# Moving half of a weight's decode from the last first product into the attention loop

## The chip, the cores and the metric

The kernel runs on one core of a Trainium2 chip. The metric is the device time of one execution in microseconds (us), as a median over several runs. The core has a matmul engine (PE, with its weight loads shown as PEld), a vector engine (DVE), an activation engine (ACT), a general engine (POOL) and a queue engine (SP), which here issues all the DMA transfers. The engines run side by side, each works through its own list in order, and they wait for each other by semaphores. Matmuls write into PSUM; everything else lies in SBUF, and the large intermediates lie in device memory.

## The reference

Thresholded attention (8 batches, 8 heads, 576 positions, head size 64), then a gated two-layer product over its output (4608 rows of 512, inner width 2048):

```python
scores = scale * np.matmul(q, k.transpose(0, 1, 3, 2))
thresh = np.max(scores, axis=-1, keepdims=True) - tau
scores = np.where(scores >= thresh, scores, -1000000000.0)
attn = np.exp(scores - np.max(scores, axis=-1, keepdims=True))
attn = attn / (np.sum(attn, axis=-1, keepdims=True) + 1e-09)
x = np.matmul(attn, v)      # heads side by side: (4608, 512)
h = x @ w_in                # (4608, 2048)
sp = np.where(h > 20.0, h, np.log1p(np.exp(np.minimum(h, 20.0))))
g = h * np.tanh(sp)
out = g @ w_out             # (4608, 512)
```

The function from `h` to `g` is Mish, which ACT has as one function. The two weights reach the chip as 64-bit floating-point numbers, viewed as integers, and are turned into 32-bit ones on the chip.

## The kernel before, in words

**Splitting.** Most products are made of 32-bit numbers split into a high part `hi`, rounded by ACT, and a low part `lo = x - hi`, subtracted by DVE or POOL. A product then takes three matmuls: high by high, high by low, low by high.

**Decode** (class `Decode`, lines 111 to 150). A piece of a weight is 128 rows by 256 columns (`WC`). `load` fetches the 64-bit words, 256 KB. `first` makes two ACT steps of 256 columns; `clamp` and `shift` are one DVE step each; `sign` is a third one on DVE; `add` is an integer add on POOL. Then the value is whole. `upper` rounds it to the high half (ACT), `lower` subtracts (DVE or POOL). `w_in` has 32 pieces, `w_out` has 32 as well: 16 rows of pieces (`NF`), two column halves.

**The attention loop** (from line 528) goes over 288 tiles of 128 rows of scores (`NT`), nine to a pair of heads. In its step `g` it issues, for each engine in the order in which the lines stand:
- `begin(g + 1)`: the score matmuls of the next tile, into one of two PSUM buffers `s`
- the products with `v` of an earlier tile, and ACT's copies of tile g - 3 (`evacuate_hi`)
- on DVE `row_max` of tile g, small steps, `lo_main` of tile g - 3, and, where g is even, `tail_lo`
- on ACT the exponential
- on POOL `normalise` of tile g - 1
- on DVE `masked`, the last reader of the PSUM buffer of scores of tile g, which the scores of tile g + 2 need
- `advance(stream, n)`: n matmuls of the first product (`x @ w_in`) of the batch before, n by the tables `MIX...`
- `transposes(g - 2)`.

Work that isn't tied to a tile is put into this order by lists. `weights` holds the pieces of `w_in`; in the steps that `W1_STEPS` names a piece is taken into `decoding`, and from then on each step issues its next entry: two empty ones (`LAG`), `first`, then the entries that `spread` lays out by `STAGES`, then `upper` and `lower`. An entry of three has its first part issued behind `lo_main`, its second ahead of `masked`, its third behind `masked` (from tile 39 on, `JOIN`). The 32 pieces of `w_in` are all taken by step 48. InOrder (line 77) keeps the order of each engine as written.

**The first product** (`gemm1`, line 440) makes `h` for half a batch (288 columns) and 128 inner rows in twelve matmuls, into one of two PSUM buffers shared with the products with `v`. A copy brings it to `hst`, four of them go to device memory in one store (`hd`); there are two `hst` buffers. For the batches ahead of the last, ACT copies; for the last batch (B - 1), DVE. After the last tile five steps of the loop drain (`DRAIN` matmuls of the product in each).

**The last first product** (lines 661 to 717) stands behind the loop. It has 32 units of 12 matmuls (`UNIT`, 384 in all). `decode_step(u)` is called ahead of each unit and issues the steps of all 32 pieces of `w_out`, a piece a unit, six pieces in flight. Four of the six homes lie in the large buffer `four`, two in small ones. In units 9, 11, 13 and 15 a quarter of `h` of chunk 0 (256 columns) goes through `gate`: ACT's Mish, ACT's rounding, POOL's subtraction, of 1024 columns each. Large buffers come from a pool of four of 16 KB (`slot`), small ones from a pool of two of 4 KB (`small`).

**The second product** (from line 737) goes over ten chunks of columns of `h`, the first and the last shorter, and in each over four output blocks `d` (`o`, 48 matmuls each); `d` 0 and 1 need the first column half of `w_out`, 2 and 3 the second. While a chunk is multiplied, the next ones are loaded and gated (`make_g`). Its matmuls aren't bound to the written order, and some of the first chunk's are placed among those of the last first product.

Of the kernel before, what the change touches and what calls it, by code (L numbers as in the profile page):

```python
# [7 lines left out]
U32 = mybir.dt.uint32  # L8
# [8 lines left out]
NP = H // 2  # L17
LOADS = ((1, 0, 1, 3, 2, 3, 7, 3, 5, 8), (0, 3, 3, 2, 5, 4, 5, 8, 5, 7), (0, 0, 2, 4, 5, 4, 7, 6, 7, 8))
W1_STEPS = (1, 3, 4, 6, 7, 8, 10, 12, 13, 15, 16, 17)
STAGES = ((0, 1, 1), (0, 1, 1))  # L20
THIRD = ((),)
LAG = 2
XSPLIT = (4, 1, 2)
# [11 lines left out]
HB = S // 2  # L35
NBLK = 2 * B
NC = 512
CHUNKS = (0, *range(256, B * S, NC), B * S)
QCOL = {
    0: [(0, 0)],  # L40
# [20 lines left out]
MIX = (11, 12, 6, 9, 8, 13, 12, 14, 16, 6, 16, 4, 12, 4, 15, 5, 16, 13)  # L61
MIX_FIRST = (11, 12, 6, 9, 8, 13, 6, 14, 22, 6, 16, 4, 12, 4, 15, 9, 16, 13, 7, 12, 5, 10, 8, 13, 12, 14, 16, 6, 16, 4, 12, 4, 15, 5, 16, 13)
MIX_LAST = (12, 14, 16, 6, 16, 4, 12, 4, 15, 5, 16, 13, 11, 12, 6, 9, 8, 13, 12, 14, 16, 6, 16, 4, 12, 4, 15, 5, 16, 13, 11, 12, 6, 9, 8, 13)
DRAIN = 24
LAST = {1: 0, 4: 1, 6: 2, 8: 3}
WIDTH = (256, 320, 320, 256)
XOFF = (0, 256, 256, 0)
# [85 lines left out]
def attention_moe(tc, q, k, v, tau, w_in, w_out, out):  # L153
# [3 lines left out]
    with ExitStack() as outer:  # L157
        dram = outer.enter_context(tc.tile_pool(name="dram", bufs=1, space=DRAM))
        cst = outer.enter_context(tc.tile_pool(name="cst", bufs=1, side="left"))
        psh = outer.enter_context(tc.tile_pool(name="psh", bufs=2, space=PSUM))  # L160
        hd = [dram.tile([P, NF, HB], F32, name=f"hd{i}") for i in range(NBLK)]

        ident = cst.tile([P, P], F32, name="ident")
# [6 lines left out]
        with ExitStack() as first:  # L170
# [6 lines left out]
            with ExitStack() as att:  # L177
# [11 lines left out]
                def spread(work, steps):  # L189
                    middle = [[skip] * 3 for _ in range(steps[2] + 1)]  # L190
                    for i, made in enumerate((work.clamp, work.shift, work.join)):
                        middle[steps[i]][i] = made
                    return middle

                def decode_w1(d, j):
                    sl = slice(j * WC, (j + 1) * WC)
                    st = dec.tile([P, 4 * WC], U32, name="dec")
                    half, at = divmod(j * WC, DF // 2)
                    hi, lo = (w[:, d, at:at + WC] for w in w1[half])
                    work = Decode(nc, st, hi, lo)  # L200
                    work.load(w_in[d * P:(d + 1) * P, sl])
                    if d + j * ND in ONV:
                        middle = [skip] * 3
                        middle[ONP] = lambda: work.lower(nc.vector)
                        last = [(work.upper,), middle]
                    else:
                        last = [(lambda: (work.upper(), work.lower(nc.gpsimd)),)]
                    return [(work.first, skip), *spread(work, STAGES[(d + j) % 2]), *THIRD, *last]

                def prep(pi):  # L210
                    full = pi < FULL
# [228 lines left out]
                def gemm1(b, xs):  # L440

                    halves = (range(NF // 2), range(NF // 2, NF))
                    if b < B - 1:
                        order = [(c, fs) for c in range(2) for fs in halves]
                    else:
                        order = [(c, fs) for fs in halves for c in range(2)]
                    for c, fs in order:
                        for f in fs:
                            h = psh.tile([P, 512], F32, name="h", tag="ph")
                            half, at = divmod(f * P, DF // 2)  # L450
                            i = 0
                            for d in range(ND):
                                xh, xl = xs[d][c]
                                wh, wl = (w[:, d, at:at + P] for w in w1[half])
                                for a, m in ((wh, xh), (wh, xl), (wl, xh)):
                                    nc.tensor.matmul(h[:, :HB], a, m, start=i == 0, stop=i == 3 * ND - 1)
                                    i += 1
                                    if i < 3 * ND:
                                        yield
                            if f % 4 == 0:  # L460
                                hst = xpool.tile([P, 4, HB], F32, name="hst", bufs=2)
                            if b < B - 1:
                                nc.scalar.copy(hst[:, f % 4], h[:, :HB])
                            else:
                                nc.vector.tensor_copy(hst[:, f % 4], h[:, :HB])
                            if f % 4 == 3:
                                nc.sync.dma_start(hd[2 * b + c][:, f - 3:f + 1, :], hst)
                            yield
# [5 lines left out]
                NPAIRS = B * NP  # L474
                NT = NPAIRS * 9
                weights = [lambda d=d, j=j: decode_w1(d, j) for j in range(DF // WC) for d in range(ND)]
                decoding = []
                pairs = {}
                tiles = {}
# [48 lines left out]
                for g in range(NT + 5):  # L528
# [71 lines left out]
                        chores.setdefault(max(g + 2, 2), []).append(work())  # L600
                    if weights and g % 18 in W1_STEPS:
                        decoding.append([()] * LAG + weights.pop(0)())
                    if g < NT:
                        if g < JOIN:
                            for work in now:
                                if len(work) == 3:
                                    work[2]()
                        if g % 2 == 0:
                            both = sm.tile([P, 2 * S], F32, name="p", bufs=2)
                        tiles[g]["both"] = both  # L610
                        half = both[:, :S] if g % 2 == 0 else both[:, S:]
                        tiles[g]["p"] = masked(g, tiles[g]["s"], tiles[g]["st"], tiles[g]["e"], half)
# [20 lines left out]
            def slot(pool, shape, kind, n):  # L633

                return pool.tile(shape, kind, name="g", tag="g", bufs=n)

            def small(kind, shape):
                return wr.tile(shape, kind, name="ht", tag="ht", bufs=2)

            def load_h(ht, c, fs):  # L640

                at, end = CHUNKS[c], CHUNKS[c + 1]
                while at < end:
                    i, off = divmod(at, HB)
                    m = min(HB - off, end - at)
                    to = at - CHUNKS[c]
                    nc.sync.dma_start(ht[:, :, to:to + m], hd[i][:, fs, off:off + m])
                    at += m
# [6 lines left out]
            def quarter(k):  # L655
                return slice(4 * k, 4 * k + 4)
# [3 lines left out]

            n0 = CHUNKS[1]
            w2 = [weights2(wr, 0)]
            four = slot(wr, [P, 4, 4 * WC], U32, 4)
            h0 = slot(wr, [P, NF, n0], F32, 4)
            g0 = [slot(wr, [P, NF, n0], F32R, 4) for _ in "hl"]
            work = {}

            def fetch(i):
                if i < 2 * NF:
                    st = four[:, i % 6] if i % 6 < 4 else small(U32, [P, 4 * WC])  # L670
                    work[i] = Decode(nc, st, None, None)
                    j, f = divmod(i, NF)
                    work[i].load(w_out[f * P:(f + 1) * P, j * WC:(j + 1) * WC])

            def decode_step(u):

                if (i := u - 3) in work:
                    work[i].first()
                if (i := u - 5) in work:
                    j, f = divmod(i, NF)  # L680
                    work[i].hi, work[i].lo = (w[:, f] for w in w2[j])
                    work[i].upper()
                if (i := u - 4) in work:
                    work[i].clamp()
                    work[i].shift()
                    work[i].sign()
                    work[i].add()
                if (i := u - 5) in work:
                    work.pop(i).lower(nc.vector if i % 2 else nc.gpsimd)
                    fetch(i + 6)  # L690

            for i in range(6):
                fetch(i)
            for k in range(4):
                load_h(h0[:, quarter(k)], 0, quarter(k))
            for _ in stream:
                pass
            stream = gemm1(B - 1, batches[B - 1])
            UNIT = 12
            for u in range(NF * 2):  # L700
                if u == NF + 2:
                    early.close()
                    er = second.enter_context(tc.tile_pool(name="er", bufs=1, side="right"))
                    w2.append(weights2(er, 1))
                decode_step(u)
                if u in (9, 11, 13, 15):
                    k = (u - 9) // 2
                    gate(h0[:, quarter(k)], *(g[:, quarter(k)] for g in g0), nc.gpsimd)
                if u == NF + 2:
                    h1 = slot(wr, [P, 8, NC], F32, 4)  # L710
                    for k in range(2):
                        load_h(h1[:, quarter(k)], 1, quarter(k))
                advance(stream, UNIT)
            for u in range(NF * 2, NF * 2 + 5):
                decode_step(u)
            for _ in stream:
                pass

# [83 lines left out]
```

## Time and profile before

| | us |
|---|---|
| median of 3 runs | 1405.22 |
| the runs | 1408.76, 1405.22, 1402.37 |
| the profiled execution | 1407.83 |
| its span (first to last instruction) | 1406.0 |

The mean granted clock of PE over the span is 0.982 of full speed.

| engine | busy us | share | instructions |
|---|---|---|---|
| PE | 1370.3 | 97% | 8798 |
| DVE | 1008.2 | 72% | 2992 |
| ACT | 947.1 | 67% | 2098 |
| POOL | 774.1 | 55% | 1107 |

A row of the timeline has the start in us, the length in us, the engine, the line (L87 is a helper through which all instructions of the ordered engines pass, so they are told apart by the names of their tiles), the operation, what is written from what is read, the shapes, and how many in a row were merged. In brackets stands for how long the engine had been idle, and what released it. Names in the trace: `g` and `ht` are also the homes of the pieces of `w_out`, since they come from those two pools; `dec` are the homes of pieces in the loop; `w2h` and `w2l` are the split second weight; `p<-s,st,e` on DVE is `masked`.

### The profile page before, as it was taken

What the parts mean: (1) busy time and instruction counts of PE and PEld (TensorE: products, weight loads), DVE (VectorE), ACT (ScalarE), POOL (GpSimd) and SP (SyncE); (2) the same over time, 40 slices, a digit from 0 to 9 for tenths busy, and PEclk for the clock granted to TensorE, in tenths of its full rate; (3) what the DMA queues carried; (4) which work ended last, traced back from release to release, by engine and by line L of the source; (5) the groups of instructions that cost most, each with busy time, mean ns of one, the idle gap of its engine ahead of it and who ended that gap; (6) DMA issues with size and microseconds to landing.
All of it is one profiled execution on the core that took longest, in us unless ns stands there. A gap on an engine that the chain in (4) does not pass through costs nothing.

```text
span 1406.0 us, 27557 instructions
## 1 busy us (share of the span) xinstructions
PE 1370.3 (97%) x8798; PEld 1234.7 (88%) x8798; DVE 1008.2 (72%) x2992; ACT 947.1 (67%) x2098; POOL 774.1 (55%) x1107
## 2 busy tenths in 40 slices
PE   8999899999999999999999999988899999999999
PEld 5555789999999999999999999987888888888888
DVE  4899999999999999999999999949934222322210
ACT  3778878888888888888888888746655333433310
POOL 3678888788788787787787887636500000000000
PEclk6999899999999999999999999998999999999999
DMA  4334323233333233232333332155656334544210
GB/s 131 90 89 114 111 83 122 91 108 105 99 96 113 91 117 108 91 117 91 112 101 100 99 113 88 59 200 160 207 148 164 116 112 121 143 109 116 83 53 29
DMA packets 121599, 154.62 MB, mean 110 GB/s; under 512 B 23152, under 2 KB 100976, under 8 KB 121456
## 3 DMA queue, kind: packets, MB, share of 16 engines
q1 hardware_dynamic: 121456, 152.87, 35.8%
q8 instruction: 70, 1.15, 0.3%
q14 instruction: 73, 0.60, 0.1%
HBM read 105.64 MB, written 47.19 MB: 109 GB/s over the span
## 4 chain that ended last, share of the span: by engine, by line
PE 88%; DVE 5%; ACT 3%; DMA 2%; issue 2%; POOL 0%; SPq 0%; POOLq 0%; ACTq 0%; DVEq 0%
PE o L751 27%; PE h L87 25%; PE s L87 14%; PE y L87 12%; PE tp L87 9%; PE t L87 1%; DVE g L87 1%; DVE st L87 1%; DVE p L87 1%; DVE ht L87 1%; DVE dec L87 1%; DMA g<-hd 1%; DMA g<-w_out 1%; ACT e L87 1%; DVE hst L87 0%
## 5 line engine op out<-in xcount | busy, mean ns | idle before, releaser
L751 PE MATMUL o<-g,w2h 128*128 128x512 f32 (+1 forms) x1280 | 367.5, 372 | 1.9 <-POOL g L87 1.9
L87 PE MATMUL h<-xh,w1h 128*128 128x288 f32 x1024 | 305.2, 298 | 9.2 <-DVE hst L87 8.3
L87 PE MATMUL h<-xl,w1h 128*128 128x288 f32 x1024 | 304.8, 298 | 0.5 <-POOL xl L87 0.5
L87 PE MATMUL h<-xh,w1l 128*128 128x288 f32 x1024 | 304.5, 297 | 0.0
L87 POOL TENSOR_SCALAR p<-p,st 128x576 f32<-128x576 f32 x288 | 245.0, 851 | 66.5 <-DVE st L87 40.4
L751 PEld LDWEIGHTS o<-g,w2h 128*128 128x128 f32 x1280 | 234.1, 190 | 45.7 <-POOL g L87 2.1
L87 PE MATMUL s<-k,q 128*128 128x288 f32 (+1 forms) x1280 | 260.2, 329 | 12.2 <-DVE p L87 10.8
L87 DVE SCALAR_TENSOR_TENSOR p<-s,st,e 128x576 f32<-128x576 f32 x288 | 235.0, 816 | 23.5 <-ACT e L87 13.8
L751 PE MATMUL o<-g,w2l 128*128 128x512 f32 (+1 forms) x640 | 238.2, 372 | 3.7 <-POOL w2l L87 3.7
L87 ACT ACTIVATE e<-s,st 128x576 f32<-128x576 f32 x288 | 214.4, 744 | 36.1 <-DVE st L87 29.0
L87 DVE TENSOR_REDUCE st<-s 128x1 f32<-128x576 f32 x288 | 216.5, 752 | 12.1 <-PE s L87 12.0
L87 PEld LDWEIGHTS s<-k,q 128*128 128x128 f32 (+1 forms) x1280 | 185.0, 192 | 44.0 <-DVE p L87 23.7
L87 DVE TENSOR_TENSOR lo<-tp,hi 128x512 fp32r<-128x512 f32 (+1 forms) x280 | 174.7, 632 | 50.7 <-ACT hi L87 43.8
L87 PEld LDWEIGHTS h<-xh,w1h 128*128 128x128 f32 x1024 | 195.1, 191 | 11.5 <-DVE hst L87 10.3
L87 PEld LDWEIGHTS h<-xl,w1h 128*128 128x128 f32 x1024 | 194.8, 190 | 0.7 <-POOL xl L87 0.7
L87 PEld LDWEIGHTS h<-xh,w1l 128*128 128x128 f32 x1024 | 195.0, 190 | 0.0
L653 DVE TENSOR_TENSOR g<-ht,g 128x1024 fp32r<-128x1024 f32 (+1 forms) x68 | 78.4, 1162 | 148.1 <-ACT g L652 148.1
L87 PE MATMUL tp<-ident,p 128*128 128x128 f32 x1152 | 176.7, 276 | 3.5 <-DVE lo L87 2.3
L87 ACT CAST hi<-tp 128x512 fp32r<-128x512 f32 (+1 forms) x280 | 149.8, 546 | 35.1 <-PE tp L87 32.2
L87 PEld LDWEIGHTS tp<-ident,p 128*128 128x128 f32 x1152 | 140.4, 141 | 15.1 <-issue 8.0
L651 ACT ACTIVATE ht<-ht 128x1024 f32<-128x1024 f32 (+1 forms) x68 | 68.5, 1009 | 126.4 <-DMA ht<-hd 126.4
L751 PEld LDWEIGHTS o<-g,w2l 128*128 128x128 f32 x640 | 121.9, 191 | 25.9 <-POOL w2l L87 3.9
(69 smaller groups left out, 2211.5 us busy)
## 6 DMA issues: line engine op xcount, KB each, us to landing
hd<-hst SPq DMA_DIRECT2D x64, 576.0 KB, 3.3
r<-q SPq DMA_DIRECT2D x120, 160.0 KB, 2.3
r<-k SPq DMA_DIRECT2D x120, 160.0 KB, 2.3
ht<-hd SPq DMA_DIRECT2D x60, 288.0 KB, 3.2
r<-v SPq DMA_DIRECT2D x56, 160.0 KB, 2.3
dec<-w_in SPq DMA_DIRECT2D x32, 256.0 KB, 2.8
out_t<-ost SPq DMA_DIRECT2D x32, 256.0 KB, 2.8
g<-w_out SPq DMA_DIRECT2D x22, 256.0 KB, 3.8
```

The costliest lines, as they stand in the source:

```text
L87: made = method(*args, **kwargs)
L651: nc.scalar.activation(ht, ht, AF.Mish)
L653: engine.tensor_tensor(gl, ht, fv(gh), ALU.subtract)
L751: nc.tensor.matmul(o[:, :m], a, b, start=n == 0, stop=n == 3 * NF - 1)
```

## The change

- The pieces of the second column half of `w_out` are decoded in the attention loop. Once `w_in` is done, a piece is taken in each step that 14 divides (56 to 266). Clamp, shift and sign with add are laid two steps apart (`STAGES[2]`). The whole 32-bit value isn't split there but stored in device memory (`w2d`).
- The last first product decodes the 16 pieces of the first half alone, eight in flight, four in five units (`PACE`), one unit sooner relative to their load. The homes are two large buffers.
- The quarters of `h` of chunk 0 lie in the two small buffers, so that the third and fourth are loaded after the first and second gate. The gates stand in units 12, 15, 18 and 21 (`GATES`).
- In unit 18 the stored half of the weight is loaded in four parts of 512 KB, and in units 24, 26, 28 and 30 (`SPLITS`) split in steps of 1024 columns: ACT rounds, POOL and DVE subtract by turns. The load of `h1` moves from unit 18 to unit 24.
- In the last batch's first product, ACT copies every second `h`, DVE the others.
- `DRAIN` is 18 instead of 24.

```diff
-STAGES = ((0, 1, 1), (0, 1, 1))
+W2_STEP = 14
+STAGES = ((0, 1, 1), (0, 1, 1), (0, 2, 4))
+PACE = {(5 * f) // 4: f for f in range(NF)}
+GATES = (12, 15, 18, 21)
+SPLITS = (24, 26, 28, 30)
-DRAIN = 24
+DRAIN = 18
...
+        w2d = dram.tile([P, NF, WC], F32, name="w2d")
...
+                def decode_w2(f):
+                    st = dec.tile([P, 4 * WC], U32, name="dec")
+                    work = Decode(nc, st, None, None)
+                    work.load(w_out[f * P:(f + 1) * P, WC:])
+
+                    def last():
+                        nc.sync.dma_start(w2d[:, f], fv(work.a))
+
+                    return [(work.first, skip), *spread(work, STAGES[2]), (last,)]
...
-                            if b < B - 1:
+                            if b < B - 1 or f % 2:
                                 nc.scalar.copy(hst[:, f % 4], h[:, :HB])
...
+                weights2 = [lambda f=f: decode_w2(f) for f in range(NF)]
...
+                    elif not weights and weights2 and g % W2_STEP == 0:
+                        decoding.append([()] * LAG + weights2.pop(0)())
...
-            four = slot(wr, [P, 4, 4 * WC], U32, 4)
-            h0 = slot(wr, [P, NF, n0], F32, 4)
+            homes = []
+            for _ in range(2):
+                four = slot(wr, [P, 4, 4 * WC], U32, 4)
+                homes += [four[:, i] for i in range(4)]
...
+                if (f := PACE.get(u - 2)) is not None:
+                    work[f].first()
+                if (f := PACE.get(u - 4)) is not None:
+                    work[f].upper()
+                if (f := PACE.get(u - 3)) is not None:
+                    work[f].clamp()
+                    work[f].shift()
+                    work[f].sign()
+                    work[f].add()
+                if (f := PACE.get(u - 4)) is not None:
+                    work.pop(f).lower(nc.vector if f % 2 else nc.gpsimd)
+                    if f < 8:
+                        fetch(f + 8)
+
+            def fetch_h0(k):
+                h0[k] = small(F32, [P, 4, n0])
+                load_h(h0[k], 0, quarter(k))
...
                 if u == NF + 2:
                     early.close()
                     er = second.enter_context(tc.tile_pool(name="er", bufs=1, side="right"))
                     w2.append(weights2(er, 1))
+                    raw2 = slot(wr, [P, NF, WC], F32, 4)
+                    for k in range(4):
+                        nc.sync.dma_start(raw2[:, quarter(k)], w2d[:, quarter(k)])
                 decode_step(u)
-                if u in (9, 11, 13, 15):
-                    k = (u - 9) // 2
-                    gate(h0[:, quarter(k)], *(g[:, quarter(k)] for g in g0), nc.gpsimd)
-                if u == NF + 2:
+                if u in GATES:
+                    k = GATES.index(u)
+                    gate(h0[k], *(g[:, quarter(k)] for g in g0), nc.gpsimd)
+                    if k < 2:
+                        fetch_h0(k + 2)
+                if u == 24:
                     h1 = slot(wr, [P, 8, NC], F32, 4)
                     for k in range(2):
                         load_h(h1[:, quarter(k)], 1, quarter(k))
+                if u in SPLITS:
+                    k = SPLITS.index(u)
+                    hi, lo = (w[:, quarter(k)] for w in w2[1])
+                    nc.scalar.copy(hi, raw2[:, quarter(k)])
+                    (nc.vector if k % 2 else nc.gpsimd).tensor_tensor(lo, raw2[:, quarter(k)], fv(hi), ALU.subtract)
                 advance(stream, UNIT)
-            for u in range(NF * 2, NF * 2 + 5):
-                decode_step(u)
```

More of the change, by code (lines that the diff above doesn't have):

```diff
@@ L662, in attention_moe @@
             w2 = [weights2(wr, 0)]
-            four = slot(wr, [P, 4, 4 * WC], U32, 4)
-            h0 = slot(wr, [P, NF, n0], F32, 4)
+            homes = []
+            for _ in range(2):
+                four = slot(wr, [P, 4, 4 * WC], U32, 4)
+                homes += [four[:, i] for i in range(4)]
             g0 = [slot(wr, [P, NF, n0], F32R, 4) for _ in "hl"]
             work = {}
[L668 to L673, printed above, removed]
@@ L675, in decode_step @@
-            def decode_step(u):
[L677 to L695, printed above, removed]
+            h0 = {}
+            def fetch(f):
+                work[f] = Decode(nc, homes[f % 8], *(w[:, f] for w in w2[0]))
+                work[f].load(w_out[f * P:(f + 1) * P, :WC])
+            def decode_step(u):
+                if (f := PACE.get(u - 2)) is not None:
[11 more added lines that the diff above has]
+                        fetch(f + 8)
@@ L696, in attention_moe @@
+            def fetch_h0(k):
+                h0[k] = small(F32, [P, 4, n0])
+                load_h(h0[k], 0, quarter(k))
+            for f in range(8):
+                fetch(f)
+            for k in range(2):
+                fetch_h0(k)
             for _ in stream:
@@ L699, in attention_moe @@
             UNIT = 12
-            for u in range(NF * 2):
+            for u in range(2 * NF):
                 if u == NF + 2:
```

## The prediction

> **What bounds the kernel now.** I read the page's forty slices first, then the busy time by stages, then the waits and the timeline of the bad stretch.
>
> ```profile
> PE   8999899999999999999999999988899999999999
> 500.00:550.00 50.00, 49.99 (x385) 49.28 (x384) 45.84 (x152) 42.90 (x103) 39.88 (x61) 1.00 0.33 107
> 900.00:950.00 50.00, 45.35 (x335) 44.13 (x334) 30.63 (x87) 26.86 (x67) 19.54 (x29) 0.98 0.44 154
> 950.00:1000.00 50.00, 43.23 (x289) 41.56 (x287) 44.06 (x85) 32.89 (x72) 31.75 (x33) 0.91 0.58 197
> 1000.00:1050.00 50.00, 46.11 (x261) 41.15 (x261) 31.26 (x47) 28.09 (x40) 10.90 (x12) 0.93 0.55 149
> 1050.00:1100.00 50.00, 50.00 (x219) 40.84 (x218) 17.28 (x16) 26.22 (x25) 0.00 (x0) 1.00 0.58 159
> ```
>
> TensorE (PE) is the bound nearly everywhere. It is full in the attention loop (500 to 550) and in the second product (from 1050), and it has a hole between about 925 and 1026, where the last batch's first product shares the engines with the decode of the second weight. So what is saved in the hole shortens the kernel, and a wait newly put on PE in the loop lengthens it. The columns of a window row are the length, PE, weight load, DVE, ACT, POOL, clock, DMA share and GB/s.
>
> How large is the hole?
>
> ```profile
> 909.06 2.12 PE h L87 x16
> 929.54 0.41 PE L87 MATMUL h<-xl,w1h 128*128 128x288 f32 x1 [0.48 <-POOL xl L87]
> 1003.55 0.40 PE L751 MATMUL o<-g,w2h 128*128 128x256 f32 x2
> 1003.91 0.40 PE L751 MATMUL o<-g,w2h 128*128 128x256 f32 x2
> 1017.39 0.58 PE L751 MATMUL o<-g,w2l 128*128 128x256 f32 x1 [3.73 <-POOL w2l L87]
> 1026.43 0.64 PE L751 MATMUL o<-g,w2h 128*128 128x512 f32 x2
> ```
>
> An unhindered `h` matmul takes 2.12/16 = 0.1325 us. Three `o` matmuls of 256 columns lie between 1003.55 and 1003.91, 0.12 us each. At 929.54 ten of the last first product's 384 matmuls are out: 374 x 0.1325 = 49.6 us are left, then the first chunk of the second product, 192 x 0.12 = 23.0 us. Without a wait the first 512-wide matmul would start at 929.5 + 72.6 = 1002.1; it starts at 1026.4. The hole costs 24.3 us.
>
> What fills it is the order on DVE, here over two units of twelve matmuls:
>
> ```profile
> 981.57 0.42 DVE L87 TENSOR_TENSOR w2l<-g,w2h 128x256 fp32r<-128x256 f32 x1
> 981.90 0.45 DVE L87 COPY hst<-h 128x288 f32<-128x288 f32 x1
> 982.27 0.78 DVE L87 TENSOR_SCALAR ht<-ht 128x256 f32<-128x256 f32 x2
> 983.09 0.43 DVE L87 SCALAR_TENSOR_TENSOR ht<-ht 128x256 uint32<-128x256 uint32 x1
> 983.43 0.45 DVE L87 COPY hst<-h 128x288 f32<-128x288 f32 x1
> 983.80 1.51 DVE L87 TENSOR_SCALAR g<-g 128x256 f32<-128x256 f32 x2
> 985.34 0.42 DVE L87 SCALAR_TENSOR_TENSOR g<-g 128x256 uint32<-128x256 uint32 x1
> 985.68 0.42 DVE L87 TENSOR_TENSOR w2l<-ht,w2h 128x256 fp32r<-128x256 f32 x1
> 964.59 2.40 POOL L87 TENSOR_TENSOR g<-g 128x1024 fp32r<-128x1024 f32 x1
> 964.78 2.48 DVE L87 SCALAR_TENSOR_TENSOR ht<-ht 128x256 uint32<-128x256 uint32 x1
> ```
>
> The pattern repeats after 985.68 - 981.57 = 4.11 us. DVE is never idle in it, while PE needs 24 x 0.1325 = 3.18 us: the product runs at DVE's pace. The last two rows are a gate: while POOL subtracts 1024 columns, a DVE step that takes 0.42 us takes 2.48 us, about 2.1 us more. There are four of these. The hole closes with the 3.73 us in which PE waits for the last decoded piece (`w2l`).
>
> **The change part by part.** *The hole.* Sixteen of the 32 pieces leave it. By the rows two pieces cost DVE 4.11 us less two copies of 0.37 us (start to next start), 3.37 us, so 1.69 us a piece. Sixteen take 27.0 us; half of the copies stay on DVE, ten of them while pieces run, 3.75 us; four gates on POOL still hold DVE by 2.1 us, 8.4 us. That is 39.2 us over the units 3 to 22, for which PE needs 20 x 1.59 = 31.8 us. So DVE still sets the pace there, but by some 7 us. The nine units behind carry only wide steps (four splits, one a unit or two) and run at PE's pace.
>
> New waits. The gate's two ACT steps now stand ahead of ACT's odd `hst` copies, for which PE's next PSUM bank waits:
>
> ```profile
> 949.07 1.28 ACT L87 ACT_TABLE_LOAD   x1
> 950.37 1.06 ACT L87 ACTIVATE g<-g 128x1024 f32<-128x1024 f32 x1
> 951.46 1.05 ACT L87 CAST g<-g 128x1024 fp32r<-128x1024 f32 x1
> ```
>
> Only the first of the four has the table load; I take 1.3 us for it, and 1.5 us for copies held behind `upper`, which waits for POOL (bounds: nothing, if ACT runs ahead of PE; 3.4 us, all three rows, for each of two gates). On SP's queue the reload of `h0` waits for a gate's end, with `hst` stores behind it, but the buffer of a store is due only some units later: nothing. The raw loads and the `h1` load put two blocks of 2 MB among the stores in the DMA queues. Before, such a block of `h0` loads made DVE wait for a store once:
>
> ```profile
> 947.41 0.46 DVE L87 COPY hst<-h 128x288 f32<-128x288 f32 x1 [2.32 <-DMA hd<-hst]
> ```
>
> I take nothing for it, as the stores then due are few, and 2.3 us at most for each block.
>
> The 3.73 us wait goes, as half of the second weight needs only splits from unit 24 on. The drain with 18 instead of 24 matmuls a step keeps five more as cover for the last pair's chain, 5 x 0.13 = 0.7 us gained. New hole: 7 + 1.3 + 1.5 = 9.8 us; gain 24.3 - 9.8 + 0.7 = **15.2 us** (9 to 20).
>
> *The loop.* Each of 16 pieces brings two ACT steps, clamp, shift and sign on DVE, one add on POOL, a load and a store. The first weight's decode shows their durations in the loop:
>
> ```profile
> L87 ACT ACTIVATE dec<-dec 128x256 f32<-128x256 f32 x25 | 10.8, 432 | 0.0
> L87 DVE TENSOR_SCALAR dec<-dec 128x256 f32<-128x256 f32 x25 | 11.8, 472 | 0.0
> L87 DVE TENSOR_SCALAR dec<-dec 128x256 uint32<-128x256 uint32 x26 | 13.7, 527 | 0.1
> L87 DVE SCALAR_TENSOR_TENSOR dec<-dec 128x256 uint32<-128x256 uint32 x26 | 18.7, 718 | 0.4
> L87 POOL TENSOR_TENSOR dec<-dec 128x256 uint32<-128x256 uint32 x26 | 19.8, 762 | 3.3 <-DVE dec L87 2.7
> ```
>
> On DVE that is 0.47 + 0.53 + 0.72 = 1.72 us a piece. DVE has idle time (45.84 of 50 busy), but it isn't where the pieces land. g % 14 with stages 0, 2, 4 puts all three on even tiles: clamp and shift ahead of `masked`, sign behind it. Scores two tiles later need the PSUM that `masked` frees:
>
> ```profile
> 498.73 0.82 DVE L87 SCALAR_TENSOR_TENSOR p<-s,st,e 128x576 f32<-128x576 f32 x1
> 499.61 0.79 PE L87 MATMUL s<-k,q 128*128 128x288 f32 x4
> 307.85 0.82 DVE L87 SCALAR_TENSOR_TENSOR p<-s,st,e 128x576 f32<-128x576 f32 x1
> 309.46 0.79 PE L87 MATMUL s<-k,q 128*128 128x288 f32 x4
> ```
>
> In the first pair PE starts 0.06 us after DVE's end: what is put ahead of `masked` there delays PE by its length. In the second there are 0.8 us to spare. Followed through one period of eighteen tiles, seven of nine even tiles are like the first pair (0.06 to 0.15 us) and two like the second; odd tiles have 0.2 to 0.7 us, which take most of the sign. What a piece costs in all, the end of the first weight's decode shows, against the same nine tiles when it is over:
>
> ```profile
> 161.10 0.38 PE L87 MATMUL s<-k,q 128*128 128x288 f32 x1
> 195.03 0.40 PE L87 MATMUL s<-k,q 128*128 128x288 f32 x1 [1.63 <-DVE p L87]
> 278.23 0.40 PE L87 MATMUL s<-k,q 128*128 128x288 f32 x1
> 305.71 0.38 PE L87 MATMUL s<-k,q 128*128 128x288 f32 x1
> ```
>
> 33.93 against 27.48 us, less 0.5 us for four more matmuls in one tile: 5.9 us for some 5.5 pieces, 1.1 us a piece, with an `upper` on ACT and a `lower` on POOL that the new pieces don't have. I take 0.9 us: 16 x 0.9 = **14.4 us**. Bounds: 0.5 us a piece (clamp and shift unblocked, 0.28 us each, on seven of nine tiles), 8 us; 1.25 us, 20 us. POOL's add and the DMAs find slack of a tile or more and cost nothing; if POOL's cover went, `normalise` would reach PE's transposes late.
>
> The Trainium skill, "SBUF — State Buffer", section "SBUF: two separate sides", says that DVE in a two-port mode, or with two SBUF inputs, and GpSimd hold their shared ports as an exclusive lock for a whole instruction, and the loser blocks fully. The gate's pair of rows (2.40 beside 2.48) agrees. By that rule, with POOL busy 39.88 of 50 us in steps near 0.85 us, each of three DVE steps would wait an estimated 0.34 us over its 0.28 to 0.42 us alone: 2.0 us a piece instead of 1.72, some 3 us more in all.
>
> *Sum*, against the profiled execution's 1407.8 us (span 1406.0): -15.2 + 14.4 = -0.8, 1407.0 us. It lies 2.6 us over the median of 1405.2, so I predict **1404 us**.
>
> **The rivals.**
> *A, the loop hides the pieces* (faster). DVE idles 4.2 of 50 us, 3.6 us in the 43 us of fourteen tiles, twice what a piece takes; ACT idles more. If waits elsewhere take it up, a piece costs 0.3 us, 5 us in all: -15.2 + 5 = -10, **1395 us**. Against it: the 0.06 us pairs, and nine tiles that did not hide it.
> *B, DVE's new steps are held by POOL in the loop* (slower). Most steps waited for one POOL step at the most, but the slowest didn't:
>
> ```profile
> L87 DVE TENSOR_SCALAR dec<-dec x64: 272/308/2395, 25.9 to 191.8; 128x256 f32<-128x256 f32 x32, 128x256 uint32<-128x256 uint32 x32
> ```
>
> 2.4 us is three POOL steps in a row. If one step in each piece meets such a run, a piece costs 0.9 + about 1 us, 30 us in all: -15 + 30 = +15, **1419 us**. It turns the change into a loss above 7 us once a piece costs over 1.4 us. For it: POOL's 80%. Against: the median of 308 ns.
> *C, the last product stays bound* by gates and ACT's copies, each gate holding PE 3 us more than I think: gain 5 us, +9, **1414 us**. For it: in the 4.8 us of three units ACT would have 5.5 us of work (2.4 pieces of some 1.2, a gate's 2.1, copies of 0.4). Against: the gates now lie three units apart, not two.
>
> **How the numbers follow.** Forecast 0.46, A 0.29, B 0.17, C 0.08. The forecast's own range is 1398 to 1412. The whole range goes down to 1391 (a gain of 19 with A's cost) and up to 1416, which takes in C and leaves out most of B. A measurement of this kernel can tell about 0.5%, 7 us, from no change: faster 0.29, same 0.46, slower 0.25.
>
> **What would show it.** The interval between two scores on PE in the tiles of a piece: 1 us longer per piece if right, unchanged under A, 2 us under B. The time from 929 to the first 512-wide matmul: 82 us if right, 92 under C. New waits of PE for `DVE p` between 250 and 880 us, where the view of waits has none for PE now. The 3.73 us wait for `w2l` is gone. What would make the prediction wrong above all: that waits in successive tiles overlap, or that the chain ACT, DVE, POOL, ACT of a piece is slower than DVE alone.

## The result, and the profile after

| | before | after |
|---|---|---|
| median, 18 runs each | 1401.03 us | 1408.22 us |
| fastest and slowest run | 1395.75, 1409.20 | 1402.71, 1415.92 |
| profiled execution, its span | 1407.83, 1406.0 | 1406.11, 1404.3 |
| mean granted clock | 0.982 | 0.990 |

After stands to before as 1.0054, with a 95% interval of 1.0029 to 1.0079: slower by 0.5%, some 7 us.

The two profiled executions stand the other way round, and that has to be cleared up first. The first window of the windows view (length, PE, weight load, DVE, ACT, POOL, clock, DMA share, GB/s), of before and then of after:

```profile
0.00:50.00 50.00, 43.84 (x171) 28.92 (x172) 26.06 (x105) 24.44 (x57) 21.66 (x31) 0.76 0.37 108
```

```profile
0.00:50.00 50.00, 44.39 (x209) 29.66 (x210) 33.98 (x129) 30.25 (x71) 27.70 (x39) 0.90 0.43 121
```

The first 50 us are the same work in both kernels, but this execution of after had a granted clock of 0.90 there, that of before 0.76, and it got through 209 matmuls instead of 171. What was gained so has nothing to do with the change. So I compare stretches between the same instructions. The ends of the first are the `masked` of tile 54 and that of tile 287 on DVE's timeline (start, length, engine, line, operation), before and after:

```profile
197.60 0.82 DVE L87 SCALAR_TENSOR_TENSOR p<-s,st,e 128x576 f32<-128x576 f32 x1
913.18 0.82 DVE L87 SCALAR_TENSOR_TENSOR p<-s,st,e 128x576 f32<-128x576 f32 x1
```

```profile
189.00 0.82 DVE L91 SCALAR_TENSOR_TENSOR p<-s,st,e 128x576 f32<-128x576 f32 x1
919.62 0.82 DVE L91 SCALAR_TENSOR_TENSOR p<-s,st,e 128x576 f32<-128x576 f32 x1
```

After reached tile 54 8.6 us sooner, by the start alone. From there the **loop** took 715.58 us before and 730.62 after: +15.0. The **drain**, from there to the last first product's `xl` matmul that waits for POOL, took 15.54 in both. The **hole**, from that matmul to the first 512-wide one, took 96.9 us before; after, on PE's timeline:

```profile
935.98 0.40 PE L91 MATMUL h<-xl,w1h 128*128 128x288 f32 x1 [0.47 <-POOL xl L91]
1024.93 0.40 PE L780 MATMUL o<-g,w2h 128*128 128x512 f32 x1
```

That is 88.95 us: -7.9. From there to the end both take 379.5 us, within 0.2. In sum +15.0 - 7.9 = +7.1 us, which is the difference of the medians, 7.2.

Two windows of after that answer to those shown of before:

```profile
500.00:550.00 50.00, 49.32 (x379) 48.40 (x379) 45.88 (x151) 43.10 (x106) 40.37 (x62) 1.00 0.36 112
950.00:1000.00 50.00, 39.81 (x264) 37.49 (x263) 30.62 (x53) 28.31 (x57) 27.59 (x24) 0.93 0.61 200
```

The loop (500 to 550) does 379 matmuls in 50 us where it did 385, and DVE is no fuller than before. From 950 to 1000 PE is now emptier than before (39.81 against 43.23), with DVE, ACT and POOL all far from full. That is not what an engine at its limit looks like.

The waits in the loop, 250 to 880 us, in the view of waits (engine, line, what was waited for: us in all, times, longest), before and after:

```profile
PEld s L87 <- DVE p L87: 6.8, 33, 0.3
```

```profile
PEld s L91 <- DVE p L91: 18.7, 50, 0.9
PE s L91 <- DVE p L91: 7.2, 15, 0.7
```

Before, no matmul waited there, only weight loads, by up to 0.3 us. After, scores wait for `masked` fifteen times, by up to 0.7 us. And in the hole, of before (929 to 1027) and of after (936 to 1025), the largest:

```profile
PE h L87 <- DVE hst L87: 8.3, 9, 3.1
PE o L751 <- POOL w2l L87: 3.7, 1, 3.7
PE o L751 <- POOL g L87: 1.9, 1, 1.9
```

```profile
PE h L91 <- DVE hst L91: 8.5, 7, 3.6
PE h L91 <- ACT hst L91: 1.6, 2, 1.1
PE o L780 <- ACT g L91: 0.7, 1, 0.7
```

The waits for `w2l` and for POOL's `g` are gone, 5.6 us. The waits for a copy of `h` out of PSUM are not: 8.3 us before, 10.1 after, though half of the pieces have left. The three lines add up to 13.9 us before and 10.8 after, 3.1 us less. The rest of the 7.9 us gained, some 5 us by subtraction, goes with a higher clock of the matmuls: the granted clock over the hole is 0.91 in before and 0.96 in after.

### The profile page after: what moved, and what is told of

It reads as the page before. It is cut to its first block, busy times and chain, and to the rows that moved or that the text cites. A ratio compares the mean times of both kernels' runs of the same rounds, so it can differ in the third digit from the quotient of the medians.

```text
span 1404.3 us, 27561 instructions
## 1 busy us (share of the span) xinstructions
PE 1364.3 (97%) x8798; PEld 1226.7 (87%) x8798; DVE 996.7 (71%) x2970; ACT 948.0 (68%) x2102; POOL 770.0 (55%) x1101
## 4 chain that ended last, share of the span: by engine, by line
PE 84%; DVE 7%; ACT 5%; issue 2%; DMA 1%; POOL 0%; SPq 0%; ACTq 0%; DVEq 0%
PE o L780 28%; PE h L91 23%; PE s L91 13%; PE y L91 11%; PE tp L91 8%; DVE p L91 2%; DVE dec L91 1%; DVE st L91 1%; PE t L91 1%; DVE g L91 1%; ACT e L91 1%; ACT hi L91 1%; DVE lo L91 1%; DMA hd<-hst 1%; DVE tk L91 1%
## 5 line engine op out<-in xcount | busy, mean ns | idle before, releaser
L91 PEld LDWEIGHTS h<-xh,w1h 128*128 128x128 f32 x1024 | 194.3, 190 | 13.5 <-DVE hst L91 10.2
```

Source lines behind the costliest of these rows:

```text
L91: made = method(*args, **kwargs)
```

## The experiments

All stretches are in us and begin and end at the instructions named above; the drain is 15.54 in all runs, within 0.02. The whole time of a single profiled execution is not compared, since the start moves it by up to 10 us (column "tile 54": when its `masked` ends). The last column is PE's granted clock over the hole, from the windows view.

| kernel | tile 54 | loop | hole | clock |
|---|---|---|---|---|
| before | 198.42 | 715.58 | 96.89 | 0.91 |
| after | 189.82 | 730.62 | 88.95 | 0.96 |
| loop part alone (x1) | 195.43 | 730.54 | 94.98 | 0.91 |
| hole part alone (x2) | 197.86 | 715.51 | 87.97 | 0.98 |
| gates late (x4) | 197.67 | 730.71 | 79.93 | 1.00 |
| two steps on a loose tile (x8) | 195.63 | 727.56 | 87.93 | 0.98 |
| subtraction on DVE (x3) | 197.69 | 730.37 | 81.15 | 0.98 |
| copies on DVE (x5) | 189.86 | 730.74 | 87.44 | 0.96 |
| no DVE steps (x7) | 187.96 | 716.93 | 87.79 | 0.98 |
| both cures (x10) | 194.98 | 718.14 | 78.97 | 1.00 |
| both cures, timed (x12) | 195.36 | 718.14 | 79.33 | 1.00 |
| both, and copies (x11) | 189.79 | 718.04 | 79.58 | 1.00 |
| odd tiles (x6) | 195.39 | 727.06 | 86.05 | 1.00 |

The five kernels with the same hole as after (after itself, x2, x6, x7, x8) scatter from 86.05 to 88.95 us, and they do so in the order of the clock: x6 at 1.00, then x7, x8 and x2 at 0.98 (87.79 to 87.97), then after at 0.96. All of them have the same wait of 3.6 us in the hole, but not the same clock behind it. That wait's end in x6, and the window with it:

```profile
973.15 0.40 PE L91 MATMUL h<-xh,w1h 128*128 128x288 f32 x1 [3.58 <-DVE hst L91]
973.00:979.00 6.00, 5.85 (x44) 5.85 (x45) 3.40 (x10) 4.33 (x9) 2.78 (x4) 1.00 0.85 241
```

So holes are best compared at a like clock; at unlike clocks a difference within some 3 us means nothing. Kernels with the same loop agree within 0.4 us.

### The parts apart

x1 is before with the decode in the loop added, whose result it doesn't use:

```diff
+W2_STEP = 14
+STAGES = ((0, 1, 1), (0, 1, 1), (0, 2, 4))
...
+                    elif not weights and pieces2 and g % W2_STEP == 0:
+                        decoding.append([()] * LAG + pieces2.pop(0)())
```

> The kernel before, with the sixteen pieces of the second half of w_out also decoded in the attention loop and stored, the result unused; the last first product is as before and decodes all 32 itself. Two stretches are measured: the loop stretch, from the end of masked of tile 54 to that of tile 287 (715.6 us before, 730.6 after), and the hole, from the last xl-matmul wait at the start of the last first product to the first 512-wide matmul of the second product (96.9 before, 89.0 after). Theory L (the two parts add, the loop costs 0.94 us a piece): loop stretch 730 to 731, hole 96 to 98. Rival (part of the loop's 15 us comes from something else in the change, such as where buffers lie): loop stretch under 728. Rival (the loop's pieces are hidden): 716 to 718.

x2 is after without the decode in the loop; the wide splits work on other data of the same size:

```diff
-                weights2 = [lambda f=f: decode_w2(f) for f in range(NF)]
+                weights2 = []
...
-                        nc.sync.dma_start(raw2[:, quarter(k)], w2d[:, quarter(k)])
+                        nc.sync.dma_start(raw2[:, quarter(k)], hd[0][:, quarter(k), :WC])
```

> The changed kernel without the decode of w_out's second half in the loop; in its place the four raw loads read columns of h from device memory, so the second half of the second weight is left out of the result. Theory L: loop stretch 715 to 716.5 as before, hole 88 to 90 as after, so about 1393 to 1398 us in all by the start's luck. Rival (the pieces in the loop also slow the hole, by DMA traffic or late buffers): hole under 87.

Measured: x1's loop 730.54, x2's 715.51, both as expected. x2's hole is 87.97, just under the 88 to 90 expected. x1's is 94.98, 1.9 less than before's at the same granted clock and less than the 96 to 98 expected; why isn't shown. The loop part costs 15.0 us by itself, also when the hole is decoded as in before, and the hole part gains some 8 to 9 by itself. Neither needs the other, so each can be settled alone.

### The hole: which part of it holds PE

```diff
-GATES = (12, 15, 18, 21)
-SPLITS = (24, 26, 28, 30)
+GATES = (22, 24, 26, 28)
+SPLITS = (25, 27, 29, 31)
```

> The changed kernel with the four gates of chunk 0 in units 22, 24, 26, 28 instead of 12, 15, 18, 21, and the splits in 25, 27, 29, 31: behind the decode of the first half. Theory G (the gates are what keeps the hole long: ACT's table load and two steps hold the next piece and the odd copies, then POOL's subtraction holds DVE, in a chain that PE waits for): the hole falls from 89 to 78 to 82 us, the PE waits between units 12 and 22 (10 us in all) fall under 3. Rival D (the chain of a piece itself, ACT-DVE-POOL-ACT, is too slow for four pieces in five units): hole 86 to 89, with PE waits spread over units 4 to 22. Rival E (it only moves the waits behind unit 22): 87 to 91, with waits after unit 22.

Measured: 79.93 us, 9.0 less than after. Against x6, whose clock is 1.00 as well, it is 6.1 us less; the other 2.9 are the slow clock that after has in its hole and x4 has not. With the gates behind the last piece, the same instructions cost 7.3 us over the unhindered 72.6 instead of 16.3. The waits of x4's PE in its hole:

```profile
PE h L91 <- DVE hst L91: 2.5, 5, 0.8
PE h L91 <- ACT hst L91: 1.8, 2, 1.0
```

The two big waits of after, 1.41 and 3.58 us ahead of units 16 and 17, are gone. It is neither the pieces nor the gates, but gates among pieces. How a gate does it, after's timeline shows (ACT, POOL, DVE and PE rows of the first two gates, by start; in brackets the idle time before and what ended it):

```profile
958.14 1.28 ACT L91 ACT_TABLE_LOAD   x1
959.43 1.06 ACT L91 ACTIVATE ht<-ht 128x1024 f32<-128x1024 f32 x1
960.52 1.05 ACT L91 CAST g<-ht 128x1024 fp32r<-128x1024 f32 x1
961.65 2.40 POOL L91 TENSOR_TENSOR g<-ht,g 128x1024 fp32r<-128x1024 f32 x1 [3.27 <-ACT g L91]
961.93 3.00 DVE L91 TENSOR_SCALAR g<-g 128x256 f32<-128x256 f32 x2 [1.92 <-ACT g L91]
965.31 0.45 DVE L91 COPY hst<-h 128x288 f32<-128x288 f32 x1
965.82 0.40 PE L91 MATMUL h<-xh,w1h 128*128 128x288 f32 x1 [1.41 <-DVE hst L91]
...
968.82 2.44 POOL L91 TENSOR_TENSOR g<-ht,g 128x1024 fp32r<-128x1024 f32 x1 [0.25 <-ACT g L91]
969.08 2.46 DVE L91 SCALAR_TENSOR_TENSOR g<-g 128x256 uint32<-128x256 uint32 x1
971.46 0.44 DVE L91 COPY hst<-h 128x288 f32<-128x288 f32 x1
971.96 0.61 PE L91 MATMUL h<-xh,w1h 128*128 128x288 f32 x1 [3.58 <-DVE hst L91]
```

Read it from the top. The gate takes ACT for 3.4 us; the next piece's first step stands behind it on ACT, so DVE idles 1.92 us. When DVE may go on, POOL's subtraction has begun, and DVE's two steps take 3.00 us (the pair took 0.61 a moment before, at 958.95). The PSUM copy stands behind them in DVE's order, and PE behind the copy: 1.41 us. The second gate finds DVE already late, and holds a 0.42 us step for 2.46: PE waits 3.58 us. The engines stop in turn. That is why none of them is full:

```profile
sum 89.00, PE 78.28 PEld 75.73 DVE 51.25 ACT 51.31 POOL 33.25; mean PE 8.70 PEld 8.41 DVE 5.69 ACT 5.70 POOL 3.69
```

(the windows view's sum over the 89 us of after's hole). Is it ACT's part of this chain that counts, or POOL's?

```diff
-                    gate(h0[k], *(g[:, quarter(k)] for g in g0), nc.gpsimd)
+                    gate(h0[k], *(g[:, quarter(k)] for g in g0), nc.vector)
```

> The changed kernel with the low half of each gate of chunk 0 subtracted on DVE (1.2 us for 1024 columns) instead of POOL (2.4 us, in which DVE's decode steps are held). Late gates took 9.0 us out of the hole; this asks which half of a gate does it. Theory P (POOL holding DVE for 2.1 us four times is the larger part): hole 89 to 83 to 86 us, and no DVE decode step over 1.6 us in it. Theory A (ACT's gate steps, 2.1 us each and 3.4 us for the first, hold the next pieces and the odd copies): hole stays at 87 to 89, with PE waiting for hst copies on ACT or for DVE steps that wait for ACT.

Measured: 81.15 us, 7.8 less than after, and 6.6 to 6.8 less than x7, x8 and x2 at the same clock of 0.98; theory P had said 83 to 86. With the gates where they are and the same steps on ACT, only the subtraction has gone to DVE. DVE's rows at one of these gates:

```profile
968.43 1.23 DVE L91 TENSOR_TENSOR g<-ht,g 128x1024 fp32r<-128x1024 f32 x1 [2.94 <-ACT g L91]
969.94 0.61 DVE L91 TENSOR_SCALAR g<-g 128x256 f32<-128x256 f32 x2
970.59 0.42 DVE L91 SCALAR_TENSOR_TENSOR g<-g 128x256 uint32<-128x256 uint32 x1
```

DVE does the subtraction itself in 1.23 us, half of POOL's 2.40, and its next steps have their short durations. It still idles 2.94 us for ACT, and that costs much less. So taking POOL out of the gate gives as much as moving the gates. x3 also clears POOL's own list of the 2.4 us step, so it doesn't by itself tell POOL's hold on DVE from POOL's delay of the pieces' adds. The rows above speak for the hold: PE's two waits there end with a copy that stands right behind DVE steps of 3.00 and 2.46 us.

The third candidate was ACT's copies of `h` behind the gates:

```diff
-                            if b < B - 1 or f % 2:
+                            if b < B - 1:
```

> The changed kernel with all PSUM copies of the last first product on DVE again, none on ACT. Theory A (ACT's gates hold the odd copies): the PE waits for hst on ACT (1.6 us in the trace of after) go, hole 87 to 89. Rival (sharing the copies is what keeps DVE from being the pace): DVE gets 16 x 0.37 = 6 us more, hole 91 to 95.

Measured: 87.44 us, 1.5 less than after at the same clock of 0.96, and within the 87 to 89 of theory A; the rival's 91 to 95 did not come. ACT's part in the copies makes less of a difference than one execution of each can tell.

### The loop: what a piece costs and where

x7 leaves clamp, shift and sign out; POOL's add works on what is there, and all else (ACT's steps, POOL's, the load and the store) stays.

```diff
-                    return [(work.first, skip), *spread(work, STAGES[2]), (last,)]
+                    middle = [[skip] * 3 for _ in range(STAGES[2][2] + 1)]
+                    middle[STAGES[2][2]][2] = add_alone
+                    return [(work.first, skip), *middle, (last,)]
```

> The changed kernel in which the sixteen pieces of the loop leave out clamp, shift and sign on DVE (the add takes the two ACT results as they are), so the second half of the second weight isn't decoded rightly; loads, the two ACT steps, the add on POOL and the store stay. Theory S (the loop's cost is DVE steps that overrun the slack of their tile): loop stretch 715.6 + 0 to 3 us for ACT = 716 to 719. Rival (ACT's two steps, or POOL's add, or DMA traffic cost as much): 722 or more.

Measured: loop 716.93. Of the 15.0 us, DVE's three steps make 13.7; two steps on ACT, one on POOL and 384 KB of traffic a piece (a load of 256 KB, a store of 128) make 1.35 in all. What the three steps take on DVE in after, 250 to 880 us, from the view of groups (count, busy, mean ns):

```profile
L91 DVE SCALAR_TENSOR_TENSOR dec<-dec 128x256 uint32<-128x256 uint32 x14 | 8.3, 596 | 0.0
L91 DVE TENSOR_SCALAR dec<-dec 128x256 f32<-128x256 f32 x15 | 7.8, 517 | 0.0
L91 DVE TENSOR_SCALAR dec<-dec 128x256 uint32<-128x256 uint32 x15 | 6.2, 411 | 0.2
```

0.60 + 0.52 + 0.41 = 1.52 us a piece, of which 0.86 (13.7/16) reaches PE. One tile (102) shows how, DVE's and PE's rows of before and then of after:

```profile
344.13 0.69 DVE L87 TENSOR_TENSOR lo<-tp,hi 128x512 fp32r<-128x512 f32 x1 [0.47 <-ACT hi L87]
345.47 0.82 DVE L87 SCALAR_TENSOR_TENSOR p<-s,st,e 128x576 f32<-128x576 f32 x1
346.35 0.40 PE L87 MATMUL s<-k,q 128*128 128x288 f32 x1
```

```profile
338.29 0.69 DVE L91 TENSOR_TENSOR lo<-tp,hi 128x512 fp32r<-128x512 f32 x1 [0.64 <-ACT hi L91]
338.90 0.52 DVE L91 TENSOR_SCALAR dec<-dec 128x256 f32<-128x256 f32 x1
340.06 0.82 DVE L91 SCALAR_TENSOR_TENSOR p<-s,st,e 128x576 f32<-128x576 f32 x1
340.94 0.40 PE L91 MATMUL s<-k,q 128*128 128x288 f32 x1 [0.56 <-DVE p L91]
```

`masked` starts 1.34 us behind `lo_main` before, 1.77 after, with the clamp between them; `lo_main` itself comes 0.17 later, and PE's score 0.06 behind `masked` in both. PE waits 0.56 us where it didn't wait. This tile had no slack.

Tiles differ in this. Followed through the loop, the cost of one identical piece depends on the tile (g % 18) that its clamp falls on: 0.45 us on 4, 0.53 on 0, 0.59 on 2 and 16, 0.85 on 14, 1.20 on 10, 1.36 on 6 and 12, 1.66 on 8. Seven of these tiles come up a second time, and six of them repeat within some 0.1; tile 0, the last piece, fell to 0.28. If place is what counts, odd tiles, with more slack, should be cheaper:

```diff
-                    elif not weights and weights2 and g % W2_STEP == 0:
+                    elif not weights and weights2 and g % W2_STEP == 1:
```

> The changed kernel with a piece taken one tile later, so that clamp, shift and sign fall on odd tiles, which have 0.14 to 0.65 us of slack ahead of PE's scores. Theory S, worked out tile by tile from the slacks of before (0.43 us for clamp and for shift, 0.69 for sign, each with what is left over carried into the next tile): 0.14 + 0.14 + 0.33 and 0.08 for ACT = 0.7 us a piece, loop stretch 715.6 + 11 = 725 to 729. Rival T (a piece costs about 0.94 us wherever it lands): 730 to 731.

Measured: 727.06, that is 11.5 us for sixteen pieces, 0.72 each, as theory S had it. Then x8 puts two steps of each piece on one loose tile:

```diff
-STAGES = ((0, 1, 1), (0, 1, 1), (0, 2, 4))
+STAGES = ((0, 1, 1), (0, 1, 1), {14: (0, 0, 0), 2: (0, 0, 2)})
...
-                    elif not weights and weights2 and g % W2_STEP == 0:
-                        decoding.append([()] * LAG + weights2.pop(0)())
+                    elif not weights and weights2 and g % 18 in STAGES[2]:
+                        decoding.append([()] * LAG + weights2.pop(0)(g))
```

> The changed kernel with two pieces in eighteen tiles instead of one in fourteen, so placed that clamp and shift fall on the two even tiles (0 and 6 of eighteen) at which PE starts its scores 0.7 to 0.8 us after masked has ended; sign on tile 0 or 8. Theory S (a piece costs what its DVE steps overrun the slack of the tile they land on): loop stretch 715.6 + 16 x 0.2 to 0.5 = 719 to 724. Rival T (a piece costs DVE and ACT time wherever it lands, since PE, DVE and ACT are all near full): 729 to 732.

Measured: 727.56, a miss: 0.75 us a piece. Followed as above, a piece costs 0.5 us where clamp and shift fall on tile 0 of eighteen and 1.0 us where they fall on tile 6. DVE's rows at a tile of the second kind (tile 96) say part of why:

```profile
326.74 0.54 DVE L91 TENSOR_SCALAR dec<-dec 128x256 f32<-128x256 f32 x1
327.31 0.59 DVE L91 TENSOR_TENSOR tk<-t,tk 64x128 fp32r<-64x128 f32 x2
327.93 0.49 DVE L91 TENSOR_SCALAR dec<-dec 128x256 uint32<-128x256 uint32 x1
328.46 0.82 DVE L91 SCALAR_TENSOR_TENSOR p<-s,st,e 128x576 f32<-128x576 f32 x1
```

Clamp and shift put 0.54 + 0.49 = 1.03 us ahead of `masked`, where before has 0.7 to 0.8 us of slack. That is an overrun of 0.2 to 0.3 us; what makes the rest of the 1.0 isn't shown. x10, next, has one step to a loose tile instead of two.

### Both cures together

x10 has x4's gates, and in the loop clamp, shift and sign each on another loose tile (thirteen pieces taken where g % 18 is 14; for the other three, at 54, 72 and 90, there was no such set of tiles left):

```diff
+STAGES = ((0, 1, 1), (0, 1, 1), (0, 6, 8), (0, 2, 4))
...
+                    elif not weights and weights2 and (g % 18 == 14 or g in (54, 72, 90)):
+                        decoding.append([()] * LAG + weights2.pop(0)(2 if g % 18 == 14 else 3))
...
+GATES = (22, 24, 26, 28)
+SPLITS = (25, 27, 29, 31)
```

> The changed kernel with late gates (units 22, 24, 26, 28; splits 25, 27, 29, 31) and other tiles for the loop's pieces: thirteen with clamp on tile 0, shift on tile 6 and sign behind masked of tile 8 of each eighteen, one DVE step for each tile with slack; three more with clamp, shift, sign on tiles 4, 6, 8. Two clamps on one such tile overran it (1.4 us with POOL in the way, against 0.6 to 0.7 of slack), one alone should not. Theory S: loop stretch 715.6 + 13 x 0.1 to 0.3 + 3 x 0.5 to 0.9 = 718 to 722; hole 79 to 81; so 22 to 28 us less than the sum of before's stretches plus the change's loop cost, about 1384 to 1390 us where before has 1396.6. Rival T (a piece costs about the same everywhere): loop 727 or more.

Measured: loop 718.14, hole 78.97. Sixteen pieces now cost 2.6 us instead of 15.0, with the same instructions on every engine. All of the 2.6 comes early: against before, `masked` is 2.59 us late at tile 100, by which the three pieces of the other kind are done, and 2.56 at tile 286, so the ten pieces behind it, one step to a loose tile, cost nothing that can be measured. The hole is that of x4. The same kernel was then timed:

> The kernel of the run with late gates and the loop's pieces on tiles with slack, again, now timed. By the stretches of its one look (loop 718.1 against 715.6 us, hole 79.0 against 96.9) it should be 15.4 us faster than before, ratio 0.989, and 22 us faster than the changed kernel; if those stretches give it back elsewhere, less.

Measured: median 1390.51 us of 6 runs (1383.06 to 1392.60) against 1404.26 of before on the same chip, ratio 0.9905 with a 95% interval of 0.9868 to 0.9943. By stretches it is 2.6 - 17.6 = -15.0 us, where 15.4 was expected; by medians -13.8. The view of waits over x12's loop, 250 to 880 us, and one of its windows:

```profile
PEld s L91 <- DVE p L91: 7.8, 37, 0.3
```

```profile
500.00:550.00 50.00, 49.98 (x385) 49.31 (x384) 47.02 (x155) 43.44 (x106) 40.75 (x63) 1.00 0.35 112
```

The waits are back at before's (6.8 us, 0.3 the longest), and PE does 385 matmuls in the loop's window as it did before, though DVE is busier than in after (47.02 against 45.88): the same steps, in slack that existed all along.

x11 leaves more of the late copies of `h` to DVE:

```diff
-                            if b < B - 1 or f % 2:
+                            if b < B - 1 or (f % 2 and not (c and f >= NF // 2)):
```

> The same, but in the last quarter of the last first product (where the late gates and splits stand) all PSUM copies go to DVE, which has little to do there, and none to ACT. In the one look PE waited 0.98 and 0.79 us for copies on ACT and 0.81 us for one on DVE there. Theory A (those copies are held behind ACT's gates): hole 79.0 to 76.5 to 78, time 1 to 2.5 us less. Rival (ACT's gates set the pace there by themselves): no change within 0.5 us.

Measured: hole 79.58; median 1392.13 us of 9 runs, ratio 0.9906 (0.9873 to 0.9940), so theory A's 76.5 to 78 did not come, and the time is the same as x12's. Both are faster than before by 0.9%, and all their runs lie below the fastest of after (1402.71).

## Why the prediction was wrong, step by step

The prediction said -14.5 us in the hole, -0.7 in the drain and +14.4 in the loop, no change in sum. It came out -7.9, nothing and +15.0.

**The bound** was read rightly: PE in the loop and the second product, a hole between. What either part did, it did to the stretch that was named.

**The loop, 14.4 us: right.** 15.0 measured, 0.94 us a piece against 0.9 taken. The mechanism is the one given, steps ahead of `masked` on tiles without slack, and the new waits of PE for `p` stand where it said. Its size came partly by luck: one average covered pieces that cost from 0.28 to 1.67 us. POOL's add and the DMAs, costed at nothing, took 1.35 us together with ACT's two steps.

**The step that failed is the size of the new hole**: "New hole: 7 + 1.3 + 1.5 = 9.8 us". It measured 88.95 - 72.6 = 16.3 us. The 9.8 came from adding up DVE's work over units 3 to 22 (39.2 us) and holding it against PE's 31.8, with 2.1 us for a gate, and with "the nine units behind" at PE's pace. That treats the gate as load on an engine that is always busy, and has no term for the time in which DVE itself stands still and PE waits behind it. After's DVE was busy 51.25 of 89 us. The trace gives the excess in place: 1.6 us up to unit 11, before any gate; in units 12 to 21 the 120 `h` matmuls take 27.1 us where they need 15.9, and eight early `o` matmuls 1.0, so 10.2 us are lost; 4.5 us are lost behind unit 21, nearly all of it in three waits behind the fourth gate (1.41, 1.14 and 0.95 us, each with a slow restart). So some 14 of the 16.3 us lie at the four gates or right behind them, about 3.5 us each. What the runs show to be the gates' is what goes with them: 9.0 us in x4, by place alone, and 7.8 in x3, with POOL out of the chain in which ACT, POOL and DVE stop one behind the other.

Part of the 10.2 us is the clock, which the prediction put at nothing, though its windows of before show 0.98, 0.91 and 0.93 over the hole; its 24.3 us for that hole, all put down to DVE's order and the wait for `w2l`, hold matmuls at half clock too. Two windows of after, around the wait of 3.58 us:

```profile
966.00:972.00 6.00, 2.42 (x19) 2.21 (x19) 5.77 (x8) 3.67 (x7) 4.70 (x5) 0.88 0.45 170
972.00:978.00 6.00, 6.00 (x27) 6.00 (x28) 1.55 (x5) 3.13 (x6) 1.77 (x3) 0.55 0.88 249
```

In the second PE is full and its granted clock is 0.55: behind the wait 21 matmuls start 0.24 us apart instead of 0.1325, and the first even 0.41, in all 2.5 us more. Without any of it, in x6, the hole takes 86.05 us: 13.5 us over the unhindered 72.6, still more than the 9.8.

**The drain, 0.7 us gained: wrong, and small.** It took 15.54 us in both kernels.

**What else was costed at nothing.** Splits and stores as such cost little: x4 has all four splits and all four gates in its last ten units, and a hole 9.0 us shorter. Behind the blocks of DMAs DVE waited once for a store, 0.9 us, inside the 2.3 that were the bound.

**The rivals.** A (the loop hides the pieces) was wrong for this placement, but its ground, twice the idle time that is needed, was sound: x10 finds it. What stood against A, the tiles with 0.06 us, was a property of the placement. B's time (1419) did not come, nor did its mechanism: a piece cost 0.94 us, and DVE's steps in the loop 1.52 us instead of the 1.72 taken. C was nearest for the hole. It gave 92 us where the forecast gave 82, and 88.95 came; the hole is 6.5 us longer than the forecast's 9.8, some 1.6 us a gate where C had 3, and by way of POOL (x3), not of ACT's copies (x5). It had the smallest chance of the four, 0.08.

**The rule of the Trainium skill.** "SBUF — State Buffer", section "SBUF: two separate sides", has GpSimd and DVE, in a two-port mode or with two SBUF inputs, lock each other out of their shared ports for a whole instruction. At the gates the runs agree: a DVE step of 2.46 us beside 2.44 of POOL, and 0.42 us for the same step in x3, where the subtraction isn't on POOL. For the loop the estimate worked out from it, 2.0 us of DVE a piece, was too high: 1.52.

**Luck.** The median of before was taken from three runs, and lay 4.2 us above that of eighteen. The 1408.22 measured lies within the forecast's own 1398 to 1412 only for that: laid to 1401.03, a change of -0.8 us gives some 1400, and the same range ends at 1408.

## What to carry to other kernels

Idle time of an engine is no room by itself: the same sixteen pieces cost 15.0 or 2.6 us by the tile that each step was put on, so measure the slack in front of the bounding engine tile by tile and give each loose tile one step. Where work goes through several engines in a fixed order, add up the chain in which they stop each other, not the load of the fullest. And compare stretches between the same two instructions when executions differ at the start, at a like clock.

## What the runs showed of the hardware

The start decides up to 10 us: in thirteen profiled executions the same work up to tile 54 ended between 187.96 and 198.42 us. By the granted clock over the first 50 us they fall into groups: the earliest had 0.93, the three that followed (189.8) 0.90, the five about 195.4 us 0.76, and three about 197.7 us 0.73. Before's, the latest, had 0.76, so the clock isn't all of it. Runs of one kernel spread over 13 us, more than the change is worth; whether the start makes all of that isn't shown.

A wait of PE can cost more than its length. After a wait of 1.41 us the next matmul came 1.57 us late, about 0.16 us more than the wait. And the clock can fall. In the traces' clock records every change lies on a grid of 3.41 us. Over the holes of all thirteen executions, each of the thirteen slots of that grid in which PE at full clock idled 1.87 us or more was followed by a slot at half clock, and none in which it idled 1.6 us or less. Of the three in between, with 1.74, 1.81 and 1.84 us, one was. So the same wait of 3.6 us let the clock fall in after, x2, x7 and x8, where 2.2 us or more of it lay in one slot, and not in x6, where the grid cut it into 1.84 and 1.74. The four executions with late gates have no wait over 1 us in the hole, and a clock of 1.00. A slot at half clock costs up to half of its 3.41 us.
